# Adding the softmax guard 1e-9 by a two-column reduction in a fused attention and MLP kernel

## The chip, the cores and the metric

The kernel runs on one core of a Trainium2 chip. The metric is the device time of one execution in microseconds (us), as the median of three runs. The profile is of one such execution. Engines are named as the profile names them: PE is TensorE's matrix multiplication, PEld its weight loads, DVE is VectorE, ACT is ScalarE, POOL is GpSimd and SP is SyncE, whose queue issues the transfers.

## The reference

The kernel computes a blocked attention and then two MLPs on its output. The inputs q, k and v have shape (2, 8, 768, 64) in fp32, the weights of the MLPs are 512x2048 and 2048x512.

```python
k_sum = k.reshape(B, H, nb, block, D).max(axis=3)        # block = 32
v_sum = v.reshape(B, H, nb, block, D).mean(axis=3)
scores_l = scale * q @ k.T     where |i - j| < 16, else -1e9
scores_s = scale * q @ k_sum.T + log(block)
a = exp(scores_all - max(scores_all))
a = a / (sum(a) + 1e-09)
x = a @ concat([v, v_sum])
h = x @ w_in;  g = prelu(h, alpha);   x = g @ w_out      # first MLP
h = x @ w_in2; g = h * sigmoid(h);    out = g @ w_out2   # second MLP
```

The change is in the line that divides by `sum(a) + 1e-09`.

## The kernel before, in words

The attention works in 24 groups, numbered in the list `order`. A group is one block of 256 query rows of one pair of heads. Its steps are `scores` (16 small matmuls into one PSUM tile, the scaling and masking on VectorE at L531, the row maximum on VectorE at L540), `exps` (four exponentials on ScalarE at L548, each of which also leaves its row sum in one column of the tile `sm`), `normalize` (L557 to L560), `turn` (four transposes on TensorE, a copy on ScalarE) and `values` (16 matmuls, then a copy to `xh` on ScalarE and the remainder `xl` on VectorE at L588). Once for each pair of heads and batch, `prep_k` takes block maxima of the keys (a reduction at L465, a copy at L471), and `prep_v1` takes block sums of the values (additions on GpSimd at L482, a reduction on VectorE at L485).

In `normalize`, VectorE adds 1e-9 to the four sums (L557), takes their reciprocals into `rs` (L559), and GpSimd multiplies the 128x480 exponentials by them (L560). The tiles `sm` and `rs` come from a pool with two buffers for each name.

Between these steps lies the work of the first MLP. Its weights arrive as 64-bit numbers and are converted on VectorE in three steps on 128x512 tiles (L142, L146, L149); ScalarE then rounds them to a high part (L155) and GpSimd or VectorE takes the low part (L156). Every large product is made of three matmuls, of high and low parts (L281 to L283). The activation of the first MLP has a step on VectorE at L328 and one on GpSimd or VectorE at L337; L358 copies finished sums out of PSUM. After the attention, from about 135 us on, only the MLPs are left.

The kernel gives each step a key, such as `k + AT_EXPS` or `k + AT_NORM`, and emits the steps in the order of these keys. Which instruction an engine takes next is then decided by a planner when the kernel is built (`tile.TileContext(nc, schedule_with_timeline_sim=True)`): it plays the instructions through with durations of its own, so the order on an engine can differ from the order of the code. On the chip each engine works through its list in order.

Of the kernel before, what the change touches and what calls it, by code (L numbers as in the profile page):

```python
# [10 lines left out]
F32 = mybir.dt.float32  # L11
# [3 lines left out]
ALU = mybir.AluOpType  # L15
AX = mybir.AxisListType
# [5 lines left out]
P = 128  # L22
# [15 lines left out]
def tile_blocks_attention_mlps(  # L38
# [12 lines left out]
    nc = tc.nc  # L51
# [375 lines left out]
    with ExitStack() as scope0:  # L427

        gpool.append(ctx.enter_context(tc.tile_pool(name="g1", bufs=2)))
        kv = scope0.enter_context(tc.tile_pool(name="kv", bufs=4))  # L430
        att = scope0.enter_context(tc.tile_pool(name="att", bufs=2))
        ps_s = scope0.enter_context(tc.tile_pool(name="ps_s", bufs=1, space=bass.MemoryType.PSUM))
        cst = kv.tile([P, P + 4 * NC], F32, name="cst", bufs=1)
        ident = cst[:, 0:P]
        mask = cst[:, P:]

        kt_t, vt_t, vs_t, q_t = {}, {}, {}, {}

# [104 lines left out]
        def exps(n):  # L543
            t, nm = t_t.pop(n)
            e = att.tile([P, 4, NC], F32, tag="e", name="e", bufs=3)
            sm = att.tile([P, 4], F32, tag="sm", name="sm")
            for u in range(4):
                nc.scalar.activation(  # L548
                    out=e[:, u, :], in_=t[:, u, :], func=AF.Exp, bias=nm[:, u:u + 1],
                    accum_out=sm[:, u:u + 1],  # L550
                )
            e_t[n] = e
            sums[n] = sm

        def normalize(n):
            sm, e = sums.pop(n), e_t[n]
            nc.vector.tensor_scalar(out=sm, in0=sm, scalar1=1e-9, scalar2=None, op0=ALU.add)  # L557
            rs = att.tile([P, 4, 1], F32, tag="rs", name="rs")
            nc.vector.reciprocal(out=rs.rearrange("p u o -> p (u o)"), in_=sm)  # L559
            nc.gpsimd.tensor_tensor(out=e, in0=e, in1=rs.to_broadcast([P, 4, NC]), op=ALU.mult)  # L560

        def turn(n):
# [175 lines left out]
        for k, (blk, p) in enumerate(order):  # L738
            b, j = divmod(blk, BPB)
            if j == 0:  # L740
                at(k + AT_KEYS, prep_k, b, p)
                at(k + AT_SUMS, block_sums, b, p)
                at(k + AT_MEANS, means, b, p)
            at(k, scores, k)
            at(k + AT_EXPS, exps, k)
            at(k + AT_NORM, normalize, k)
            at(k + AT_TURN, turn, k)
            at(k + AT_VALUES, values, k)
            if j == 0:
                at(k + AT_SPREAD, spread, b, p)  # L750
            if k >= NQ:
                at(k - NQ + 0.01, load_q, blk, p)
            if blk == 0:
                at(k + AT_IN, first_in, p)
# [5 lines left out]
        for p in range(NPAIR if B > 1 else 0):  # L760
            t = BATCH + p * BATCH_STEP
# [3 lines left out]
        t = idx[0, NPAIR - 1] + AT_IN  # L765
        for i, *_ in seq:
            if i >= NBLK:
                break
            t = max(t + ITEM_STEP, lastk[i] + AT_LATER)
# [12 lines left out]
    while seq:  # L782
        _, f, *a = seq[0]
        item()
        if f is in_item:
            l, ch, t0, n, _ = a[0]
# [4 lines left out]
        i = parts[at_conv[0]][0] if at_conv[0] < len(parts) else 0  # L791
        due = min(due + (0.25 if f is quad_item else 0.4), 1.0)
        if at_conv[0] < 4 * CF or due == 1.0:
            n = at_conv[0]
# [79 lines left out]
```

## Time and profile before

| what | value |
|---|---|
| median of three runs | 608.99 us (608.89 to 609.29) |
| span of the profiled execution, first to last instruction | 604.6 us |
| its own device time | not given beside its span; the median is 4.4 us above the span |
| mean granted TensorE clock | 0.994 of full speed |
| L557 (the addition), 24 times | 9.0 us, 374 ns on average |

The span is shorter than the device time by what lies before the first and after the last instruction. [...] A note such as [0.50 <-DVE t L531] says that the engine sat idle for 0.50 us before this row, until that instruction released it.

### The profile page before, as it was taken

To read this page: it belongs to the slowest core of one execution; us is meant where nothing else is said; L and a number is where in the kernel's file an instruction comes from. 1 tells how busy PE (TensorE), PEld (TensorE's weight loads), DVE (VectorE), ACT (ScalarE), POOL (GpSimd) and SP (SyncE) were. 2 spreads that over 40 slices of the span, in tenths; PEclk is the share of its full clock that TensorE was granted. 3 is DMA by queue.
4 is the path that set the end of the run, shared out by engine and by line. 5 is a ranking of instruction groups with operands and counts; after the bars stand their busy time and mean duration, and the time that the engine had idled before them with its cause. 6 is when DMAs were issued, how large, how long until landed. Compare 5 with 4: busy or idle time off the path is not lost.

```text
span 604.6 us, 8927 instructions
## 1 busy us (share of the span) xinstructions
PE 576.8 (95%) x3428; PEld 483.5 (80%) x3428; DVE 424.0 (70%) x747; ACT 277.5 (46%) x636; POOL 72.3 (12%) x69
## 2 busy tenths in 40 slices
PE   2777999999999999999999999999999999999997
PEld 1556788999888888888888888888888888888886
DVE  3899979548995484349696879885972499965312
ACT  2768977654543341424544645543621245333200
POOL 2657654232100000000000000000000000000000
PEclk9988999999999999999999999999999999999999
DMA  9958754002351040003022002333130032200112
GB/s 263 341 193 260 231 147 140 2 2 70 140 154 56 0 140 0 1 1 112 28 69 70 1 1 79 131 117 93 32 108 0 1 111 96 73 1 0 54 69 88
DMA packets 31771, 52.54 MB, mean 87 GB/s; under 512 B 2288, under 2 KB 20976, under 8 KB 31728
## 3 DMA queue, kind: packets, MB, share of 16 engines
q1 hardware_dynamic: 31728, 51.97, 27.2%
q8 instruction: 27, 0.44, 0.3%
q14 instruction: 16, 0.13, 0.1%
HBM read 48.82 MB, written 3.15 MB: 86 GB/s over the span
## 4 chain that ended last, share of the span: by engine, by line
PE 82%; DVE 9%; DMA 3%; ACT 2%; SPq 1%; issue 1%; POOL 0%; DVEq 0%; POOLq 0%
PE ps L281 27%; PE ps L282 27%; PE ps L283 27%; DVE w L146 2%; DMA y<-in_w 1%; DVE w L149 1%; DMA vs<-in_vw 1%; DVE w L142 1%; DVE t L531 1%; DVE sm L557 1%; DVE nm L540 1%; PE o L579 1%; DVE kT L465 1%; ACT e L548 1%; DMA raw<-in_w 1%
## 5 line engine op out<-in xcount | busy, mean ns | idle before, releaser
L281 PE MATMUL ps<-xh,wl 128*128 128x512 f32 (+1 forms) x352 | 127.5, 367 | 1.2 <-ACT xh L587 1.2
L282 PE MATMUL ps<-xl,wh 128*128 128x512 f32 (+1 forms) x352 | 127.9, 364 | 0.0
L283 PE MATMUL ps<-xh,wh 128*128 128x512 f32 (+1 forms) x352 | 127.4, 363 | 0.0
L282 PE MATMUL ps<-gl,wh 128*128 128x512 f32 (+1 forms) x240 | 83.3, 348 | 0.0
L283 PE MATMUL ps<-gh,wh 128*128 128x512 f32 (+1 forms) x240 | 82.9, 346 | 0.0
L281 PE MATMUL ps<-gh,wl 128*128 128x512 f32 (+1 forms) x240 | 82.5, 350 | 0.0
L336 ACT CAST gh<-g 128x512 fp32r<-128x512 f32 x96 | 59.3, 622 | 46.2 <-PE ps L283 24.2
L281 PEld LDWEIGHTS ps<-xh,wl 128*128 128x128 f32 x352 | 66.5, 191 | 12.4 <-POOL e L560 1.4
L282 PEld LDWEIGHTS ps<-xl,wh 128*128 128x128 f32 x352 | 67.3, 191 | 10.2 <-issue 0.2
L283 PE MATMUL ps<-wh,gh 128*128 128x512 f32 (+1 forms) x196 | 75.4, 385 | 0.0
L283 PEld LDWEIGHTS ps<-xh,wh 128*128 128x128 f32 x352 | 67.3, 191 | 10.1
L282 PE MATMUL ps<-wl,gh 128*128 128x512 f32 (+1 forms) x196 | 75.4, 385 | 0.0
L281 PE MATMUL ps<-wh,gl 128*128 128x512 f32 (+1 forms) x196 | 75.2, 385 | 0.1
L337 DVE TENSOR_TENSOR gl<-g,gh 128x512 fp32r<-128x512 f32 x84 | 57.5, 687 | 20.7 <-ACT gh L336 20.3
L394 DVE TENSOR_TENSOR y<-ps,y 128x512 f32<-128x512 f32 x48 | 32.8, 689 | 45.4 <-PE ps L283 45.2
L324 ACT ACTIVATE g<-ps 128x512 f32<-128x512 f32 (+1 forms) x50 | 29.0, 579 | 70.8 <-PE ps L283 69.9
L155 ACT CAST wh<-w 128x512 fp32r<-128x512 f32 x64 | 39.3, 622 | 48.0 <-DVE w L149 43.5
L328 DVE SCALAR_TENSOR_TENSOR g<-m,nal,g 128x512 f32<-128x512 f32 (+1 forms) x60 | 41.4, 705 | 25.0 <-ACT m L325 24.9
L281 PEld LDWEIGHTS ps<-gh,wl 128*128 128x128 f32 x240 | 45.2, 189 | 6.6 <-issue 0.5
L282 PEld LDWEIGHTS ps<-gl,wh 128*128 128x128 f32 x240 | 45.4, 189 | 6.1 <-POOL gl L337 0.2
L283 PEld LDWEIGHTS ps<-gh,wh 128*128 128x128 f32 x240 | 45.3, 189 | 5.6
L146 DVE SCALAR_TENSOR_TENSOR w<-raw,w 128x512 uint32<-128x512 uint32 x61 | 44.6, 741 | 0.3
(82 smaller groups left out, 867.1 us busy)
## 6 DMA issues: line engine op xcount, KB each, us to landing
raw<-in_w SPq DMA_DIRECT2D x61, 512.0 KB, 3.8
vs<-in_vw SPq DMA_DIRECT2D x16, 288.0 KB, 5.6
kT<-in_kT SPq DMA_DIRECT2D x8, 480.0 KB, 5.2
q<-in_qT SPq DMA_DIRECT2D x24, 128.0 KB, 4.1
out<-y SPq DMA_DIRECT2D x11, 256.0 KB, 2.0
y<-in_vT SPq DMA_DIRECT2D x4, 384.0 KB, 6.5
y<-in_w SPq DMA_DIRECT2D x3, 512.0 KB, 7.7
raw<-in_vT SPq DMA_DIRECT2D x4, 384.0 KB, 4.5
```

Source lines behind the costliest of these rows:

```text
L142: nc.vector.tensor_scalar(out=w, in0=high, scalar1=3, scalar2=0x3FFFFFFF, op0=ALU.logical_shift_left, op1=ALU.bitwise_and,)
L146: nc.vector.scalar_tensor_tensor(out=w, in0=high, scalar=0xC0000000, in1=w, op0=ALU.bitwise_and, op1=ALU.bitwise_or)
L149: nc.vector.scalar_tensor_tensor(out=w, in0=low, scalar=29, in1=w, op0=ALU.logical_shift_right, op1=ALU.bitwise_or)
L155: nc.scalar.copy(out=hi, in_=w)
L281: nc.tensor.matmul(ps, all_, bh, start=first, stop=False)
L282: nc.tensor.matmul(ps, ah, bl, start=False, stop=False)
L283: nc.tensor.matmul(ps, ah, bh, start=False, stop=last)
L324: nc.scalar.activation(out=g[:, j * w:(j + 1) * w], in_=ps, func=AF.Relu)
L328: nc.vector.scalar_tensor_tensor(out=g[:, at], in0=m[:, at], scalar=nal[:, f + j:f + j + 1], in1=g[:, at], op0=ALU.mult, op1=ALU.add,)
L336: nc.scalar.copy(out=gh, in_=g)
L337: (nc.gpsimd if early else nc.vector).tensor_tensor(out=gl, in0=g, in1=gh, op=ALU.subtract)
L394: nc.vector.tensor_tensor(out=at, in0=src, in1=at, op=ALU.add)
```

## The change

Three small tiles of four rows by two columns are set to 1e-9 on VectorE at the start and used in turn in place of `sm`. Each exponential writes its sum into the first column of a row, and the second keeps 1e-9. A reduction over the two columns makes the sum plus 1e-9 in `rs`, and the reciprocal is taken in place. The first column is written anew for each group, the second never again.

```diff
+        eps = [kv.tile([P, 4, 2], F32, name=f"eps{i}", bufs=1) for i in range(3)]
+        for t in eps:
+            nc.vector.memset(t, 1e-9)
...
         def exps(n):
...
-            sm = att.tile([P, 4], F32, tag="sm", name="sm")
+            sm = eps[n % 3]
             for u in range(4):
                 nc.scalar.activation(
                     out=e[:, u, :], in_=t[:, u, :], func=AF.Exp, bias=nm[:, u:u + 1],
-                    accum_out=sm[:, u:u + 1],
+                    accum_out=sm[:, u, 0:1],
                 )
...
         def normalize(n):
             sm, e = sums.pop(n), e_t[n]
-            nc.vector.tensor_scalar(out=sm, in0=sm, scalar1=1e-9, scalar2=None, op0=ALU.add)
             rs = att.tile([P, 4, 1], F32, tag="rs", name="rs")
-            nc.vector.reciprocal(out=rs.rearrange("p u o -> p (u o)"), in_=sm)
+            r = rs.rearrange("p u o -> p (u o)")
+            nc.vector.tensor_reduce(out=r, in_=sm, axis=AX.X, op=ALU.add)
+            nc.vector.reciprocal(out=r, in_=r)
             nc.gpsimd.tensor_tensor(out=e, in0=e, in1=rs.to_broadcast([P, 4, NC]), op=ALU.mult)
```

## Rows read from the trace of the kernel before

**Rows 1.** The page: span, then busy us, share and instructions of each engine.

```profile
span 604.6 us, 8927 instructions
PE 576.8 (95%) x3428; PEld 483.5 (80%) x3428; DVE 424.0 (70%) x747; ACT 277.5 (46%) x636; POOL 72.3 (12%) x69
```

**Rows 2.** Stretch: length; busy us of PE, PEld, DVE, ACT, POOL; clock, DMA.

```profile
23.29:66.20 42.91, 32.79 (x381) 26.44 (x382) 42.80 (x82) 32.63 (x118) 25.81 (x23) 0.92 0.77 238
```

**Rows 3.** Waits of PE from 64 to 140 us: total us, times, longest.

```profile
PE sc L523 <- DVE t L531: 0.5, 1, 0.5
```

**Rows 4.** DVE by line and shape, 0 to 135 us: busy us, mean ns | idle before.

```profile
L540 DVE TENSOR_REDUCE nm<-t 128x4 f32<-128x480 f32 x24 | 15.4, 641 | 0.1
...
L557 DVE TENSOR_SCALAR sm<-sm 128x4 f32<-128x4 f32 x24 | 9.0, 374 | 4.7 <-ACT e L548 4.7
...
L465 DVE TENSOR_REDUCE kT<-kT 128x24 f32<-128x768 f32 x8 | 7.5, 943 | 6.4 <-DMA kT<-in_kT 6.4
...
L485 DVE TENSOR_REDUCE vr<-raw 128x24 f32<-128x192 f32 x4 | 1.3, 332 | 0.0
```

**Rows 5.** Timeline of POOL and DVE near 47 us: start us, duration us, instruction.

```profile
46.06 1.72 POOL L156 TENSOR_TENSOR wl<-w,wh 128x512 fp32r<-128x512 f32 x1
...
46.57 0.64 DVE L540 TENSOR_REDUCE nm<-t 128x4 f32<-128x480 f32 x1
...
47.13 0.68 DVE L557 TENSOR_SCALAR sm<-sm 128x4 f32<-128x4 f32 x1
...
47.81 0.43 DVE L142 TENSOR_SCALAR w<-raw 128x512 uint32<-128x512 uint32 x1
```

**Rows 6.** Timeline of POOL and DVE from 31.8 to 34 us.

```profile
31.87 1.28 POOL L156 TENSOR_TENSOR wl<-w,wh 128x512 fp32r<-128x512 f32 x1 [0.28 <-ACT wh L155]
...
32.17 1.01 DVE L557 TENSOR_SCALAR sm<-sm 128x4 f32<-128x4 f32 x1
...
33.09 0.34 DVE L485 TENSOR_REDUCE vr<-y 128x24 f32<-128x192 f32 x1
...
33.11 0.26 POOL L682 TENSOR_SCALAR nal<-al 128x16 f32<-128x16 f32 x1
...
33.91 0.16 DVE L559 RECIPROCAL rs<-sm 128x4 f32<-128x4 f32 x1
...
34.00 0.39 DVE L142 TENSOR_SCALAR w<-raw 128x512 uint32<-128x512 uint32 x1
```

**Rows 7.** Timeline of POOL and DVE from 51.4 to 54 us.

```profile
51.45 1.99 POOL L482 TENSOR_TENSOR raw<-raw 128x384 f32<-128x384 f32 x2
...
52.92 0.55 DVE L557 TENSOR_SCALAR sm<-sm 128x4 f32<-128x4 f32 x1
...
53.38 0.41 DVE L588 TENSOR_TENSOR xl<-o,xh 128x256 fp32r<-128x256 f32 x1
...
53.72 0.22 DVE L471 COPY kT<-kT 128x144 f32<-128x144 f32 x1
```

**Rows 8.** The chain that ended last, 56 to 83 us: start, us on it, what.

```profile
56.24 0.38 DVE sm L557
...
59.14 0.69 DVE sm L557
...
73.40 0.88 DVE sm L557
...
81.37 1.19 DVE sm L557
```

**Rows 9.** The first instruction on DVE, in its timeline.

```profile
4.66 0.95 DVE L465 TENSOR_REDUCE kT<-kT 128x24 f32<-128x768 f32 x1 [4.66 <-DMA kT<-in_kT]
```

**Rows 10.** Timeline of POOL and DVE, 73 to 76 us.

```profile
73.08 1.17 POOL L560 TENSOR_TENSOR e<-e,rs 128x480 f32<-128x480 f32 x1
...
75.28 0.16 DVE L557 TENSOR_SCALAR sm<-sm 128x4 f32<-128x4 f32 x1
...
75.34 0.65 DVE L540 TENSOR_REDUCE nm<-t 128x4 f32<-128x480 f32 x1
```

## The prediction, made before the changed kernel had run

> **What bounds the kernel now.** I read the page first: TensorE is busy for 576.8 of 604.6 us [rows 1], so whatever VectorE saves can only pay where TensorE waits. So I next asked in which stretch it waits, by the table of busy time per stretch. From 23.3 to 66.2 us VectorE is busy for 42.80 of 42.91 us and TensorE for only 32.79: VectorE sets the pace there, and TensorE has 10.1 us of gaps to give back [rows 2]. The list of TensorE's waits from 64 to 140 us then has one entry, 0.5 us of scores (L523) for the masking at L531, which empties their PSUM tile [rows 3]. The reader is to see that a microsecond saved on VectorE before 66 us can shorten the run by as much, and that later savings together can give 0.5 us. The three changed lines of the attention lie in the first 130 us, so nothing after that changes but its start.
>
> Then the changed line itself, in the list by line and shape: the 24 additions on 128x4 numbers take 9.0 us, 374 ns each [rows 4], far more than the 0.16 us that one takes undisturbed [rows 10]. The timeline shows why: at 47.13 the addition takes 0.68 us and ends when GpSimd's subtraction ends (46.06 + 1.72 = 47.78), although it moves four numbers [rows 5]. The same at 32.17 (it ends at 33.18, GpSimd at 33.15) [rows 6]. I found eight such additions, at 32, 47, 53, 56, 59, 69, 73 and 81 us; the other 16 show no such wait, and the one in rows 10, 0.16 us, stands for them. Their excess is 9.0 - 24 x 0.16 = 5.2 us [rows 4, 10].
>
> **The change part by part.** *The reduction for the addition.* The trace has no reduction over eight numbers, so I fit the three sizes that it has: 332 ns for 192, 641 for 480, 943 for 768 [rows 4]. Both steps are 1.05 to 1.07 ns per element, so eight elements come to 332 - 184 x 1.06 = 137 ns (an estimate from these rows), against 160 for the addition: no loss. The bounds are the addition's own 0.16 us from above and nothing from below. On the path only start to start counts, 0.06 us for the addition [rows 10], so I put the difference at zero.
>
> [...]
>
> *Does a reduction wait for GpSimd?* The row maximum at 46.57 lies wholly inside GpSimd's 46.06 to 47.78 and takes 0.64 us, its mean [rows 4, 5]. The addition right behind it waits. I therefore take the reduction's wait as zero; if it waited as the addition does, the change would give nothing.
>
> *What each freed wait is worth.* This is the step where I had to choose, because a freed wait can be taken over by the next instruction that GpSimd holds up. I went through what follows each of the eight.
>
> At 32.17: the next are the reduction L485 (33.09), a row maximum and the reciprocal (33.91), and only then the weight conversion L142 (34.00). By then GpSimd is through (33.15). All start 33.09 - (32.17 + 0.06) = 0.86 us earlier. L142 would begin at 33.14 and could meet GpSimd's small L682 (33.11 to 33.37), so the bounds are 0.6 and 0.86; I take 0.85 [rows 6, 10].
>
> At 47.13: L142 stands next, and conversions are held up by GpSimd too. It would start 0.6 us earlier and wait until the same 47.78. Worth 0, at most 0.6 [rows 5].
>
> At 52.92: next is L588, which reads PSUM and was not held up though it began before GpSimd was through (53.38, against 51.45 + 1.99 = 53.44), then the copy L471 at 53.72. L588 moves by 53.38 - 52.98 = 0.40; the copy would come at 53.32 but GpSimd runs until 53.44. So 53.72 - 53.44 = 0.28; bounds 0 and 0.40 [rows 7].
>
> At 56 and 59: the copy L471 stands right behind, and takes over the wait. Worth 0; at most 0.32 and 0.63, the time on the chain less 0.06 [rows 8, 10].
>
> At 69, 73 and 81: TensorE waits no more after 64 us but for 0.5 us [rows 3]. The chain runs through the additions at 73 and 81 for 0.88 and 1.19 us [rows 8], and their excess of 1.9 us covers both these 0.5 us and what is needed so that TensorE's earlier arrival doesn't open a new gap. Worth 0.5, bounds 0 and 0.5.
>
> *The rest.* Three memsets come before the first transfer lands: VectorE sits idle until 4.66 us [rows 9]. Even at 0.16 us each they fit ten times over; without that cover they would cost 0.5 us. The reciprocal reads another tile, of the same size: 0. Three tiles in place of two for the sums can only free ScalarE earlier: 0. One new wait: the reduction now writes `rs`, so it must wait until GpSimd's multiplication of two groups before has read that buffer, where the addition didn't. Queued behind it on VectorE would be the next row maximum, and behind that ScalarE's exponentials. The tightest of the 24 is the addition at 75.28, whose multiplication ended at 73.08 + 1.17 = 74.25 [rows 10]: 1.03 us of slack, so 0.
>
> **The sum.** 0.85 + 0.28 + 0.50 = 1.63 us. The span would go from 604.6 to 603.0, the median from 608.99 to 607.4 (the 4.4 us around the span stay). By the bounds: 0.6 us at least (608.4) and 0.86 + 0.6 + 0.40 + 0.32 + 0.63 + 0.5 = 3.3 at most (605.7). A measurement of this kernel can tell about 0.2%, 1.2 us, from no change.
>
> **The rivals.** (1) *The wait only changes its owner.* VectorE's conversions, copies and activation steps share something with GpSimd, and what starts earlier meets the same GpSimd instruction. That is what happens at 47, 56 and 59 in my own reading; if it also eats the gain at 32 and 53, because GpSimd's multiplications, released by earlier reciprocals, come earlier too and hold up L142 and L146, nothing is left but part of the 0.5: 608.7, within the bound. [...]
>
> (2) *The planner deals out the work differently: slower.* The code emits L557 and L559 one after the other, but L485 lies between their starts at 32.17 and 33.91 [rows 6], so the order was made at the build, and new durations and the earlier claim on `rs` can change it. The place is VectorE's list from 23 to 66 us. The price of one weight conversion put ahead of scores that TensorE waits for is its length there: 0.39 us for the shortest step, some 1.7 us for three (0.39, and twice about 0.65, the size of the 128x480 operations of rows 4 and 5 as an estimate). Decisive from two such swaps on, 3.4 us: less the 1.6 gained, 610.8; one leaves 609.1.
>
> (3) *More is freed than I count*, since a start shifted by 0.85 us changes every later meeting with GpSimd, and the moved waits may not be met again: up to 3.3 us by the bounds, 605.7, and 603.8 if all 5.2 us of excess lay on the path. TensorE's 10.1 us of gaps would allow it [rows 2]; the copies and conversions directly behind speak against it.
>
> **How the numbers follow.** My forecast, a gain of 0.6 to 2.4 us (0.86 + 0.6 + 0.40 + 0.5, with the moved waits at 56 and 59 left at zero), gets 0.45; rival 1 gets 0.20, rival 2 gets 0.22 and rival 3 gets 0.13. Of the forecast about three quarters lie beyond 1.2 us. Faster: 0.34 + 0.13 = 0.47. Same: 0.11 + 0.18 of rival 1 + 0.05 of rival 2 (one swap) = 0.34. Slower: 0.17 of rival 2 + 0.02 of rival 1 = 0.19. The likeliest case alone reaches from 606.6 to 608.4; for 8 in 10 I go down into rival 3, to 605.6, and up into rival 2, to 610.3.
>
> **What would show it.** Right: the reductions take about 0.14 us in all 24 cases, also beside GpSimd; the instructions after the one near 32 us start 0.85 us earlier; the copies and conversions that follow the ones near 47, 56 and 59 last longer by about what the addition waited; TensorE's idle time up to 66 us falls by about 1.1 us; memsets lie before 4.66 us. Wrong: reductions that are as long as the additions were, another order on VectorE before 66 us with longer waits of TensorE for scores or transposes, or a TensorE that waits after 66 us for more than half a microsecond.

## The result, and the profile after

The change makes the kernel slower: 612.15 us (median of 12 runs, 608.85 to 616.28) against 609.11 us (median of 12 runs in the same comparison). The ratio is 1.0055, with a 95% interval of 1.0032 to 1.0077. The prediction was 607.4 us and faster; the time lies outside its range of 605.6 to 610.3.

The page and the grouped list of VectorE after:

```profile
span 611.5 us, 8935 instructions
PE 579.4 (95%) x3428; PEld 484.9 (79%) x3428; DVE 418.4 (68%) x750; ACT 277.8 (45%) x636; POOL 72.3 (12%) x69
```

```profile
L562 DVE TENSOR_REDUCE rs<-eps 128x4 f32<-128x8 f32 x24 | 3.6, 151 | 4.7 <-ACT e L551 4.7
```

The profiled execution took 613.28 us on the device with a span of 611.5, so 1.8 us lie around the span. The local mechanism worked: the 24 reductions take 3.6 us where the additions took 9.0 [rows 4], and VectorE as a whole is busy for 5.6 us less than before [rows 1]. Yet the span is 6.9 us longer. Where did it go? First VectorE's stretch that answers to [rows 2], with the same columns:

```profile
23.29:66.20 42.91, 30.62 (x343) 23.88 (x339) 37.60 (x78) 30.66 (x110) 28.73 (x26) 0.83 0.79 234
```

VectorE is no longer full: 37.60 of 42.91 us. It waits, and so does TensorE (343 matmuls in the stretch, 381 before). The waits of TensorE from 0 to 23 us show for what (total us, times, longest), and the list of VectorE's from 0 to 100 us the same. After:

```profile
PE sc L526 <- DVE kT L468: 5.7, 1, 5.7
PE sc L526 <- DMA q<-in_qT: 4.4, 1, 4.4
```

```profile
DVE kT L468 <- DMA kT<-in_kT: 8.3, 4, 3.7
DVE w L142 <- DMA raw<-in_w: 4.7, 2, 3.7
...
DVE w L142 <- DMA y<-in_w: 1.7, 2, 1.3
```

Of the kernel before, these lists hold no wait of TensorE for q, but in its place one of 3.3 us for VectorE's block sums, and for VectorE's three entries this:

```profile
PE sc L523 <- DVE vr L485: 3.3, 1, 3.3
```

```profile
DVE kT L465 <- DMA kT<-in_kT: 6.4, 3, 4.7
...
DVE w L142 <- DMA y<-in_w: 0.6, 1, 0.6
...
DVE w L142 <- DMA raw<-in_w: 0.2, 1, 0.2
```

So VectorE waits longer for transfers, although the change issues none. The chain that ended last ran through transfers already before (start, us on it, what):

```profile
8.69 6.82 DMA vs<-in_vw
15.52 7.75 DMA y<-in_w
...
75.95 3.81 DMA raw<-in_w
```

In the changed kernel it spends longer on them:

```profile
15.21 8.78 DMA vs<-in_vw
...
25.50 10.23 DMA raw<-in_w
...
80.84 7.39 DMA raw<-in_w
```

The list of transfers has their size and the median time from issue to landing. Before:

```profile
vs<-in_vw SPq DMA_DIRECT2D x16, 288.0 KB, 5.6
...
q<-in_qT SPq DMA_DIRECT2D x24, 128.0 KB, 4.1
```

After:

```profile
vs<-in_vw SPq DMA_DIRECT2D x16, 288.0 KB, 7.6
...
q<-in_qT SPq DMA_DIRECT2D x24, 128.0 KB, 5.9
```

What vs, q and kT have in common is the pool `kv`. The change takes its three tiles of 32 bytes (per partition) from it ahead of kT, q and vs, and pushes those 96 bytes further. In the built programs q and vs started at multiples of 256 bytes before, at 256 within 512; after, at 352. In the traces the instructions keep their order on TensorE (3428 matmuls), GpSimd and SyncE; on VectorE one weight conversion changed places with its neighbour, and on ScalarE one cast (a rounding copy) with its.

### The profile page after: what moved, and what is told of

It is laid out like the page before. It is cut to its first block, busy times and chain, and to the rows that moved or that the text cites. A ratio compares the mean times of both kernels' runs of the same rounds, so it can differ in the third digit from the quotient of the medians.

```text
span 611.5 us, 8935 instructions
## 1 busy us (share of the span) xinstructions
PE 579.4 (95%) x3428; PEld 484.9 (79%) x3428; DVE 418.4 (68%) x750; ACT 277.8 (45%) x636; POOL 72.3 (12%) x69
## 4 chain that ended last, share of the span: by engine, by line
PE 85%; DMA 6%; DVE 4%; issue 1%; SPq 1%; ACT 1%; POOL 0%; POOLq 0%; DVEq 0%
PE ps L281 27%; PE ps L282 27%; PE ps L283 27%; DMA raw<-in_w 3%; DMA kT<-in_kT 2%; PE o L583 2%; DMA vs<-in_vw 1%; PE sc L526 1%; PE pt L570 1%; DVE w L146 1%; SPq L463 1%; DVE w L142 1%; DVE w L149 1%; ACT vs L498 0%; DVE nm L543 0%
## 5 line engine op out<-in xcount | busy, mean ns | idle before, releaser
L551 ACT ACTIVATE e<-t,nm 128x120 f32<-128x120 f32 x96 | 36.8, 388 | 18.1 <-DVE nm L543 13.6
```

The source lines that it names most:

```text
L551: nc.scalar.activation(out=e[:, u, :], in_=t[:, u, :], func=AF.Exp, bias=nm[:, u:u + 1], accum_out=sm[:, u, 0:1],)
```

## The experiments

Theory 1: the loss is the new place of tiles that transfers fill. Theory 2: it comes from the reduction, its new wait or the moved conversion. The ratios are to the kernel before, measured on the same chip, with a 95% interval in brackets.

**1. The tiles without their use**, and **2. their use without the shift.**

```diff
 # e1: the kernel before, with
+        eps = [kv.tile([P, 4, 2], F32, name=f"eps{i}", bufs=1) for i in range(3)]
+        for t in eps:
+            nc.vector.memset(t, 1e-9)
 # e2: the change, with
-        eps = [kv.tile([P, 4, 2], F32, name=f"eps{i}", bufs=1) for i in range(3)]
+        eps = [att.tile([P, 4, 2], F32, name=f"eps{i}", bufs=1) for i in range(3)]
```

> The kernel before with the three small tiles set up in the same pool and place as in the change, but not used: sums, addition and reciprocal are as before, and every engine takes its instructions in the order of before. q and vs then start 96 bytes further on, 32 bytes past a multiple of 64, as in the changed kernel. Theory 1 (the loss is the shifted place of the tiles that transfers fill): slower than before by about 0.5 to 0.9% (612 to 614 us), the median landing of q near 5.9 us instead of 4.1 and of vs near 7.6 instead of 5.6, the first wait of TensorE for q some 4 us. Theory 2 (the loss comes from the reduction, its new wait or the one conversion that the planner moved): same as before within 0.2%, landings of before.

> The changed kernel with the three small tiles taken from the pool of the attention's temporaries, which lies behind q and vs, so that q, vs and kT keep the places of before. The reduction, its order and its waits are those of the change. Theory 1: the loss is gone, and what is left is what the prediction summed, 607.4 us (0.1 to 0.4% faster than before); q lands in 4.1 us and vs in 5.6. Theory 2: still slower by 0.3 to 0.8%.

Measured: e1 610.10 us, ratio 1.0032 (1.0014 to 1.0050), so the tiles alone make the kernel slower, by less than expected, and by less than the 0.55% of the change, whose interval overlaps. e2 608.30 us, ratio 1.0000 (0.9980 to 1.0020): with q and vs in place, the loss is gone. Theory 2 falls; but the gain that I had summed doesn't appear either. The landings were poor witnesses: vs landed in 6.6 us in e1, where I expected 7.6, and in 7.0 in e2, where I expected 5.6. So was the wait for q, since e2, which has no loss, has the longest of all:

```profile
PE sc L526 <- DMA q<-in_qT: 11.1, 2, 6.1
```

**3 and 4. Other shifts of all three tiles.**

```diff
 # the kernel before, ahead of kT, q and vs: e3 16 words (64 bytes), e4 8 words (32 bytes)
+        gap = kv.tile([P, 16], F32, name="gap", bufs=1)
+        nc.vector.memset(gap, 0.0)
```

> The kernel before with one unused tile of 64 bytes in front of kT, q and vs: they move, but q and vs stay on multiples of 64. Theory 1 in its narrow form (what counts is the place within 64 bytes): same as before within 0.2%, landings of before. A wider form (any place that is not a multiple of 256, or the mere presence of another tile and its memset): slower by 0.3 to 0.8%. Theory 2: same as before.

> The kernel before with one unused tile of 32 bytes in front of kT, q and vs: q and vs lie 32 bytes past a multiple of 64, as in the changed kernel, by a shift of another size. Theory 1 in its narrow form: slower by 0.5 to 0.9%, landings of the changed kernel. If it were the 96 bytes as such, or the places of the tiles behind: same as before. Theory 2: same as before.

Measured: e3 613.30 us, ratio 1.0079 (1.0057 to 1.0102); e4 614.15 us, ratio 1.0095 (1.0074 to 1.0116). My narrow form, that multiples of 64 are free, was wrong: 64 bytes cost about as much as 32. What was left was a coarser grid, or that any other program brings the loss.

**5 to 8. A shift of 512 bytes, vs alone, q alone, and the change filled up to 512.**

```diff
 # e5: gap as in e3, of 128 words (512 bytes)
 # e6: 8 unused words between q and vs
 # e7: 8 unused words ahead of q, 120 between q and vs
 # e8: the change, with 104 unused words behind its three tiles
+        gap = kv.tile([P, 104], F32, name="gap", bufs=1)
+        nc.vector.memset(gap, 0.0)
```

> The kernel before with one unused tile of 512 bytes in front of kT, q and vs: all three move, but each keeps its place within 512 bytes. Shifts of 32 and 64 bytes cost 0.95 and 0.79%. If the place within 256 or 512 bytes is what counts (theory 1a): same as before within 0.2%, vs landing near 5.6 us. If any other program, tile or shift brings the loss, whatever its size (theory 1b, the transfers differ from program to program for reasons outside the layout): slower by 0.3 to 0.9%.

> The kernel before with 32 unused bytes between q and vs: only vs, whose pieces of 512 bytes took most of the added packet time, moves off its place (288 instead of 256 within 512 bytes); kT and q stay. Theory 1a, by vs: slower by 0.5 to 0.95%. Theory 1a, by q or kT: same as before. Theory 1b: slower, as all others.

> The kernel before with 32 unused bytes in front of q and 480 behind it: q alone changes its place within 512 bytes; kT doesn't move and vs moves by 512. Theory 1a, by vs: same as before within 0.2%. Theory 1a, by q: slower by 0.5 to 0.95%. Theory 1b: slower, as all others.

> The changed kernel with its three tiles filled up to 512 bytes by an unused one, so that kT, q and vs keep their places within 512 bytes. Theory 1a: as the version with the tiles in the other pool, 0 to 0.3% faster than before. Theory 1b: slower by 0.3 to 0.6%, as the change. The predicted gain of 1.6 us would show as 0.27% faster.

Measured: e5 609.86 us, ratio 1.0009 (0.9982 to 1.0037); e6 613.68, 1.0071 (1.0045 to 1.0097); e7 609.45, 1.0014 (0.9993 to 1.0034); e8 608.92, 0.9995 (0.9975 to 1.0014). A different program or a shift as such costs nothing that shows; of the tiles that transfers fill, moving vs alone by 32 bytes brings the loss; moving q doesn't. (With vs moves what lies behind it, `vr` and the attention's temporaries. The temporaries moved by up to 96 bytes in e2 without a loss, and both do in e15 below.) The list of transfers of e6, where q had not moved:

```profile
vs<-in_vw SPq DMA_DIRECT2D x16, 288.0 KB, 7.9
...
q<-in_qT SPq DMA_DIRECT2D x24, 128.0 KB, 5.3
```

q is late here as well, although it hasn't moved. That vs holds it up, on the same queue (SPq), is likely but not shown by itself. e6 has an unchanged order on all engines, and none of the changed arithmetic.

Nor does TensorE's clock carry the loss. The changed kernel was granted 0.83 of it in the stretch above, the kernel before 0.92, both a mix of 1.00 and 0.50 (in slices of 1 us, before has 0.50 from 37 to 40 us and 1.00 from 41 to 53; the changed kernel has 0.50 from 48 to 54 and 1.00 from 55 to 61). But from 23 to 66 us, with the columns of [rows 2], e2 was granted less and e6 as much as before:

```profile
23.00:66.00 43.00, 32.81 (x392) 25.39 (x390) 40.70 (x83) 33.61 (x121) 29.02 (x26) 0.80 0.82 238
```

```profile
23.00:66.00 43.00, 32.32 (x384) 24.79 (x384) 40.30 (x81) 31.85 (x114) 28.56 (x26) 0.92 0.85 246
```

The first is e2, without the loss, and the second e6, with it.

**9 to 11. The grid, and a third pair for the reduction.** (Labels 11 to 13.)

```diff
 # e11, e12: the kernel before with 32 or 64 unused words (128 or 256 bytes) between q and vs
 # e13: e2 with 64 unused words there
```

> The kernel before with 128 unused bytes between q and vs: vs starts at 384 within 512 bytes, on a multiple of 128 but not of 256. So far 256 within 512 is free of loss, and 288, 320 and 352 cost 0.3 to 0.95%. If a multiple of 128 is enough: same as before within 0.2%, vs landing in 5.6 to 6.6 us. If a multiple of 256 is needed: slower by 0.5 to 0.9%, vs landing in 6.6 to 7.9 us.

> The kernel before with 256 unused bytes between q and vs: vs starts on a multiple of 512, so that none of its 512-byte pieces lies across one. If multiples of 256 are all alike: same as before within 0.2%. If a piece that lies across a multiple of 512 costs something as well: faster than before by 0.2 to 0.5%, vs landing under 5.6 us. If the place of before was a lucky one and not a rule: slower.

> The change with its three tiles behind q and vs, and vs on a multiple of 512: a third pair (with the version above) in which only the reduction differs. The predicted gain of the reduction alone: 0.27% faster than the version above. If the wait that it frees is taken up by other waits (for transfers, or for GpSimd by the next instruction): the same as the version above within 0.2%. If the reduction costs something by itself: 0.2 to 0.3% slower than it.

Measured: e11 611.54 us, ratio 1.0039 (1.0026 to 1.0052); e12 609.26, 0.9991 (0.9977 to 1.0005); e13 608.80, 0.9998 (0.9983 to 1.0013). e11 is slower by less than the 0.5 to 0.9% that I expected, but clearly so: a multiple of 128 is not enough. Of the six places tried, only the two on multiples of 256 are free of loss, and the one at a multiple of 512 is no better. All places of vs so far, with the mean time of the 9,216 packets of 512 bytes (all of them pieces of vs), worked out from the packets in each trace, and vs's landing from the list of transfers:

```
vs within 512 bytes   kernel            ratio     mean ns of a 512-byte packet   vs lands, us
256                   before            1         31.5                           5.6
256                   e5, e7            1.0009, 1.0014   33.3, 33.2              6.5, 6.1
256                   e2, e8 (change)   1.0000, 0.9995   35.9, 34.5              7.0, 6.6
0                     e12, e13 (change) 0.9991, 0.9998   33.0, 34.2              6.6, 6.4
384                   e11               1.0039    41.4                           7.7
352                   e1, the change    1.0032, 1.0055   38.0, 39.1              6.6, 7.6
320                   e3                1.0079    40.0                           7.7
288                   e4, e6            1.0095, 1.0071   43.3, 43.4              7.6, 7.9
```

The landing times of single executions overlap; the packet times don't: 31.5 to 35.9 ns on multiples of 256, 38.0 to 43.4 off them. It is no fixed price for each piece, though: of the pieces that start between 50 and 70 us, the median takes 27 ns in e6 and e11 as in e5 and e12. When a piece off the multiple is held up and when not is open.

VectorE's waits for weights (`raw` and `y`, 0 to 100 us) fall into the same two sets. They add up to 0.8 us before and 1.9 to 3.6 in the six other profiles on multiples of 256, and to 5.3 to 6.4 in the six off them. So that is the way from the place to the time, as far as it shows: pieces of vs take longer, and VectorE waits longer for the weights.

**12 to 14. vs in long pieces.** (Labels 14 to 16.)

```diff
-            t = kv.tile([NC, NSUB, P], F32, tag="vs", name="vs")
+            t = kv.tile([NC, 2, NSUB // 2, P], F32, tag="vs", name="vs")
-            nc.sync.dma_start(out=t[NB:, 0::2], in_=vw[b, p, 0])
-            nc.sync.dma_start(out=t[:WIN, 1::2], in_=vw[b, p, 1])
+            nc.sync.dma_start(out=t[NB:, 0], in_=vw[b, p, 0])
+            nc.sync.dma_start(out=t[:WIN, 1], in_=vw[b, p, 1])
 # and accordingly where ScalarE writes block means into vs and TensorE reads it; e14 in the kernel before, e15 in the change, e16 in e2
```

> The kernel before with vs laid out so that the windows of even and odd halves lie in one run of 3072 bytes per partition each, in place of six pieces of 512 bytes 512 bytes apart. The values are the same; the planner moves some instructions, so the order is not quite that of before. In the traces a packet of 512 bytes takes 31 to 43 ns on average and one of 3072 bytes about 140, so the same bytes should need a fourth to a third less time of the transfer engines. If these transfers hold up the first 100 us: faster than before by 0.3 to 1%. If VectorE alone does: same as before within 0.2%.

> The change as it stands, with vs at 352 within 512 bytes, but written in runs of 3072 bytes. If the place hurts through the 512-byte pieces: the loss goes, and it takes the time of the next version within 0.2%, below before. If the place hurts through something else (how TensorE or ScalarE reads or writes vs): it stays 0.4 to 0.7% above the next version.

> The change with its three tiles behind vs, so that vs keeps its place of before, and vs written in runs of 3072 bytes. If the transfers took up what the reduction frees: faster than the first version of this set by 0.1 to 0.3%. If the next instructions that GpSimd holds up took it: the same as the first version within 0.1%.

Measured: e14 609.70 us, ratio 1.0009 (0.9985 to 1.0033); e15 608.97, 1.0014 (0.9988 to 1.0040); e16 608.92, 1.0014 (0.9986 to 1.0041). The place no longer matters within what these intervals tell: e15, with vs at 352, takes the time of e16, with vs at 256, and the two have the same order on every engine. So it is the 512-byte pieces through which the place acts, not TensorE's or ScalarE's use of vs. (ScalarE's two sizes of writes to vs take 586 and 370 ns before and in the changed kernel alike.) e16 takes the time of e14, as it would if other waits for GpSimd took up what the reduction frees, but these intervals are too wide to rule out the summed gain of 0.27%.

My expectation that the long pieces need a fourth less time of the engines was wrong: in the traces the packets of 512 and 3072 bytes together take 18.1 + 9.0 = 27.1 us on each of 16 engines before and 26.7 in e14. Nor was the kernel faster. But that doesn't show what long pieces are worth, because the planner gave e14 another order on all five engines, and its VectorE waits 5.8 us for weights, against 0.8 before.

## Why the prediction was wrong

**The step that failed** stands under *The rest*: "Three tiles in place of two for the sums can only free ScalarE earlier: 0." I asked of the tiles only when they are written and read, not where they lie. Their place ahead of vs costs 0.3 to 0.6% (e1 and the change itself), against nothing when vs stays on a multiple of 256 (e2, e8, e13). vs is written in pieces of 512 bytes, and at the four places off a multiple of 256 a piece takes 38 to 43 ns on average instead of 32 to 36. The price is paid ahead of the 19th normalization (112.4 us in the changed kernel), where transfers are already on the path: from there to the end the changed kernel takes 499.1 us, as the kernel before does. Later transfers come late with vs, as q (5.9 us against 4.1) and the weights in `y` (8.4 against 7.7); the median of the weights in `raw` doesn't (3.6 against 3.8), though VectorE waits longer for them. None of the three rivals was this one. Rival 2 had the right side for another reason, and its mechanism, a dealt-out order, is refuted: e4 and e6 keep the order of before on every engine and are slower, e2 and e8 have the order of the change and are not.

Why the border lies at multiples of 256 bytes no run shows. Long pieces show no loss off it (e15, with vs at 352, 1.0014, as e16 with vs at 256). q's pieces of 1024 bytes show none either: in e7, with q at 288, the packets of this size, nearly all of them q's, take 53.7 ns on average, as in e5 with q at 256. Nor does a piece of 512 bytes take longer the further it starts past a multiple: 43.3 and 43.4 ns at 32 bytes (e4, e6), 41.4 at 128 (e11).

**The reduction** went as the step on it said: 151 ns on average where I estimated 137, at most 161 in any of the 24, and no wait for GpSimd. **The fate of the freed waits** can be followed in the pair e5 and e8, where kT, q and vs lie alike. VectorE in e5:

```profile
35.20 0.15 DVE L559 TENSOR_SCALAR sm<-sm 128x4 f32<-128x4 f32 x1
...
49.61 0.67 DVE L559 TENSOR_SCALAR sm<-sm 128x4 f32<-128x4 f32 x1
50.29 0.43 DVE L142 TENSOR_SCALAR w<-raw 128x512 uint32<-128x512 uint32 x1
...
55.42 0.56 DVE L559 TENSOR_SCALAR sm<-sm 128x4 f32<-128x4 f32 x1
55.89 0.41 DVE L590 TENSOR_TENSOR xl<-o,xh 128x256 fp32r<-128x256 f32 x1
...
58.67 0.46 DVE L559 TENSOR_SCALAR sm<-sm 128x4 f32<-128x4 f32 x1
59.05 0.22 DVE L473 COPY kT<-kT 128x144 f32<-128x144 f32 x1
```

and in e8:

```profile
34.48 0.14 DVE L564 TENSOR_REDUCE rs<-eps 128x4 f32<-128x8 f32 x1
...
48.97 0.14 DVE L564 TENSOR_REDUCE rs<-eps 128x4 f32<-128x8 f32 x1
49.65 0.43 DVE L142 TENSOR_SCALAR w<-raw 128x512 uint32<-128x512 uint32 x1 [0.53 <-POOL wl L156]
...
54.77 0.15 DVE L564 TENSOR_REDUCE rs<-eps 128x4 f32<-128x8 f32 x1
54.84 0.41 DVE L594 TENSOR_TENSOR xl<-o,xh 128x256 fp32r<-128x256 f32 x1
...
57.62 0.15 DVE L564 TENSOR_REDUCE rs<-eps 128x4 f32<-128x8 f32 x1
57.69 0.46 DVE L476 COPY kT<-kT 128x144 f32<-128x144 f32 x1
```

The eighth normalization (49 us) and the tenth (58 us) are the moved waits that I forecast: the conversion idles 0.53 us for the same GpSimd instruction, and the copy takes 0.46 us instead of 0.22. In before too a conversion takes longer beside GpSimd: L146 at 40.91 us, begun during GpSimd's L156 (40.34 to 41.79), takes 1.42 us, and the one at 100.44, with GpSimd idle, 0.68. At the ninth the following L594 starts at once, 0.40 us sooner after the addition's start than in e5 (0.07 against 0.47), as said. But the largest term, 0.85 us at the fifth, had nothing to free in e5: its addition took 0.15 us there. Of the profiles with vs on a multiple of 256 that keep the addition, it waits about 1 us in before and e7, and not in e5 and e12. It hangs on whether GpSimd's subtraction (L156) starts ahead of the addition: at 31.87 against 32.17 us in before and 34.01 against 34.31 in e7, but only at 35.29 against 35.20 in e5 and 34.46 against 34.36 in e12.

How much of it reached the end shows in the start of the 5th, 15th and 19th normalization on VectorE, read from the timelines; from the 19th to the end of the span all seven take 499.0 to 499.1 us.

```
                    5th     15th    19th    5th to 15th   15th to 19th
before              32.17   73.33   105.46  41.16         32.13
e5  (addition)      35.20   75.91   108.78  40.71         32.87
e7  (addition)      34.31   75.95   108.53  41.64         32.58
e12 (addition)      34.36   74.99   107.29  40.63         32.30
e2  (reduction)     35.61   75.71   109.05  40.10         33.34
e8  (reduction)     34.48   74.42   107.24  39.94         32.82
e13 (reduction)     34.64   75.13   107.33  40.49         32.20
```

From the 5th to the 15th the reduction gains (41.04 - 40.18 =) 0.86 us on average; from there to the 19th 0.32 are given back (32.79 - 32.47), leaving 0.54 where I summed 1.63. With so few executions these are rough, and they hang on where the count starts: the 19th normalization itself starts at 107.5 us on average with the addition and at 107.9 with the reduction, no gain at all. The timed pairs say no more: medians of e2, e8 and e13 lie 0.6, 0.9 and 0.5 us under those of before, e5 and e12 in the same comparison, while the ratios in these pairs (1.0000; 0.9995 against 1.0009; 0.9998 against 0.9991) don't tell it from nothing. So the summed gain was too large by a factor of about three, or there is none. What takes the 0.32 us back was not tested. In e5 the chain of waits runs through two transfers of weights there, so that VectorE alone does not set the pace:

```profile
77.97 5.10 DMA raw<-in_w
...
87.91 4.37 DMA raw<-in_w
```

**What bounds the kernel** was therefore only half right. The step takes VectorE's full stretch from 23 to 66 us for the path and leaves out the transfers that the chain of before runs through: 6.82 and 7.75 us ahead of that stretch, and 3.81 us between the two additions at 73 and 81 us of [rows 8]. I also took the profiled execution for a typical one. By the 1.8 us that lie around a span, not the 4.4 that I worked out from the median, its own time was about 604.6 + 1.8 = 606.4, 2.7 us below the median of 609.11. Its fifth normalization starts at 32.2 us; in the other six of the table it starts at 34.3 to 35.6. How many of its waits were its own could not be seen from that one execution. The new wait on `rs`, the memsets and the reciprocal cost nothing that e2, e8 or e13 show (1.0000, 0.9995, 0.9998), as said.

No version that beats the kernel before by more than the measurement can tell was found; e2 is the change without its loss.

## What to carry to other kernels

A tile that is added to a pool moves all that lie behind it: put small tiles behind those that transfers fill, or in a pool that lies behind, and look at the addresses before and after a change. Tiles that are filled in pieces of 512 bytes should start at a multiple of 256, as far as the six places tried here show (31.5 to 35.9 ns a piece on multiples, 38.0 to 43.4 off them); check it by the mean time of such packets, because the landing times of one execution mislead (vs landed in 6.6 us in e1, with the loss, and in 7.0 in e2, without it). When the gain of an edit is a few waits of half a microsecond, look at more than one execution before summing them, since what an instruction meets on another engine changed here from one profile to the next (the fifth addition took 1.01 us in before and 0.15 in e5).

## What the runs showed of the hardware that had not been expected

The place within 256 bytes of vs, which transfers fill in pieces of 512 bytes, on an otherwise unchanged program, is worth 0.3 to 0.95% of this kernel (e1 1.0032, e4 1.0095), and 32, 64, 96 and 128 bytes past a multiple all cost (e6 1.0071, e3 1.0079, e1 1.0032, e11 1.0039). It is no fixed price for each piece: between 50 and 70 us the median piece takes 27 ns at 288 and 384 too (e6, e11). And pieces six times as long saved next to no time of the transfer engines: 27.1 us of packets on each with the 512-byte pieces in place, 26.7 without them (e14). A median execution differs from the fastest by more than the kernel's three first runs let think: 12 runs of before lay between 607.49 and 611.24 us, where the first three had spread by 0.4.
